# A side split's raw load moved to the end of the unit ahead, its store moved behind the unit's first half

## The chip, the cores and the metric

The kernel runs on one NeuronCore of one Trainium2 chip. The metric is the device time of a whole execution in microseconds, smaller being better. The kernel before took 1582.54 us (median of three runs, 1578.42 to 1582.68).

## What is computed

Windowed attention over 4 x 8 heads, 576 positions and head dimension 64 (window 64), whose output becomes a matrix x of 2304 rows by 512 columns. On it stands a mixture of eight experts, where every row goes through every expert and P holds the mixing weights, from an iterated row and column normalisation:

```python
def _moe_ref(x, w_gate, w1, w2):
    ...                                   # P: N x E, eight rounds of row and column scaling
    out = np.zeros((N, D), dtype=np.float32)
    for e in range(E):                    # E = 8
        h = np.maximum(x @ w1[e], 0.0)    # 512 -> 1024
        ye = h @ w2[e]                    # 1024 -> 512
        out += P[:, e:e + 1] * ye
    return out
```

Everything is float32. TensorE takes float32 operands as two rounded parts, a high one (the value cast to the type fp32r) and a low one (the value minus its high part); a product takes the three pairs high-high, high-low and low-high.

## The kernel before

The rows of x are worked in three passes of six tiles of 128 rows. Attention and pass 0 come first (up to about 650 us), then pass 1 and pass 2. The change is in pass 1 alone. A pass goes through 30 groups of 256 hidden columns; two groups make a unit `u` (15 units, 0 to 14).

Both matrix products of a unit are done by Strassen-like schemes of seven products on half blocks. `First` (class at L1031) is a group's product with w1, one block per group: seven steps numbered 1, 5, 6, 2, 7, 3, 4, each with six matmuls (L217). `Second` is the product with w2, two blocks per unit, `S[u][0]` and `S[u][1]`, with the same seven steps (L1160). The order of a pass is written out by hand in `flow`: F[2u+1], F[2u+2], S[u][0], S[u][1], then F[2u+3] and so on. Inside a block the steps go 6, 2, then step 1 of the next block, 7, 3, then step 5 of the next block, 4. So a unit is 28 products. Work on the other engines hangs on this order through `hook(block, step, f)`: `f` is issued right behind that step, and every engine (SP, which issues all DMAs, among them) works its own instructions strictly in the order of issue.

What hangs on it around the change:

- `load_w1` (L754), hooked on step 4 of every First block: five DMAs that refill the w1 buffer which that block has just finished with. SP waits there until TensorE is done with step 4.
- `next_pb` (L722), in every second unit: two DMAs of mixing weights, also on step 4 of a First block.
- Each unit needs seven parts of w2 (raw blocks, or sums of blocks kept in `w2d`). `load_w2` (L982) loads a part into one of four buffers `wr`; `split_w2` (L742, by `split_into`) makes the high part on ScalarE (L741) and the low part on GpSimd (L742). The load that reuses a buffer is issued just ahead of the next split, and SP waits in it for GpSimd's split of that buffer. The seven splits for the next unit, numbered 0 to 6 here, are issued at S[u][0] step 4, S[u][1] steps 6 and 2, F[2u+3] steps 1 and 5, S[u][1] step 4 and F[2u+3] step 6. The load issued with split n is the part for split n+3.
- `u2` (L1072): ScalarE's copy of bank b behind First step 6. Step 7 adds into bank b, so TensorE may not start it before that copy. It is issued behind split 5 on ScalarE.
- The side splits. In units 2 to 8 of pass 1 (`KEEP`), one part of unit 0 each is split ahead for pass 2: `load_kept` (L1002) loads the raw part into a buffer `ys`, `keep_split` (L1006 on ScalarE, L1007 on GpSimd) splits it into the second buffer `ys` and in place, `store_kept` (L1012) writes both halves to `w2keep` with two DMAs. There are two `ys` buffers, so the load of a unit reuses the buffer that the store of the unit before read. Pass 2 loads `w2keep` much later.

Of the kernel before, what the change touches and what calls it, by code (L numbers as in the profile page):

```python
# [21 lines left out]
def window_attention_sinkhorn_moe(ctx: ExitStack, tc: tile.TileContext, q, k, v, w_gate, w1, w2, out):  # L22
    nc = tc.nc
    B, H, S, D = q.shape
# [51 lines left out]
    def f32(ap):  # L76
        return ap.bitcast(F32)
# [3 lines left out]
    class Ring:  # L81
# [10 lines left out]
        def new(self):  # L92
            i = self.i % self.n
            self.i += 1
            pool = self.pool_a if i < self.na else self.pool_b
            return pool.tile(self.shape, self.dtype, tag=f"{self.name}_{i}", name=f"{self.name}_{i}")
# [226 lines left out]
    with tc.manual_schedule():  # L323
# [411 lines left out]
        def w2_block(u, part):  # L735
            e, c = groups[2 * u]
            src = w2[e, c * HD:(c + 2) * HD, :].rearrange("(g f p) (h d) -> p f g h d", g=2, f=2, h=2)
            return src[:, (1, 0, 0)[part], :, (0, 0, 1)[part], :]
# [202 lines left out]
        with ExitStack() as p3:  # L941
# [19 lines left out]
            KEEP = {u: k for u, k in zip(range(2, 9), ORDER)}  # L961
# [38 lines left out]
            def load_kept(part):  # L1000
                raw_k[part] = r = new("ys", [P, DM], F32R, 2)
                nc.sync.dma_start(out=f32(r), in_=w2_block(0, part) if part < 3 else w2d[0][:, part - 3])  # L1002

            def keep_split(part):
                r, h = raw_k.pop(part), new("ys", [P, DM], F32R, 2)
                nc.scalar.copy(out=h, in_=f32(r))  # L1006
                nc.gpsimd.tensor_tensor(out=r, in0=f32(r), in1=f32(h), op=ALU.subtract)  # L1007
                raw_k[part] = h, r

            def store_kept(part):  # L1010
                for x, t in enumerate(raw_k.pop(part)):
                    nc.sync.dma_start(out=w2keep[part][:, :, x, :], in_=f32(t))  # L1012
# [7 lines left out]
            def queue_w2(pu, ks):  # L1020
                if pu:
                    bulk.extend([lambda k=k: split_w2(*pu, ORDER[k]) for k in ks])
# [271 lines left out]
            for p, F, S, flow in plans:  # L1294
# [5 lines left out]
                def hook(blk, step, *fs):  # L1300
                    hooks.setdefault((blk, step), []).extend(fs)
# [20 lines left out]
                            hook(F[i + 3], 4, lambda p=p: next_pb(p + 1, 1))  # L1322
                for u in range(n_units - 1):
                    if p == 1 and u in KEEP:
                        hook(F[2 * u + 2], 4, lambda k=KEEP[u]: load_kept(k))
                        hook(S[u][0], 7, lambda k=KEEP[u]: keep_split(k))
                        hook(S[u][1], 2, lambda k=KEEP[u]: store_kept(k))
                    hook(S[u][0], 1, lambda s=S[u][0]: queue_w2(s.nxt, (0,)))
                    for st, k in ((1, 1), (5, 2), (6, 3), (2, 4), (7, 5), (3, 6)):
                        hook(S[u][1], st, lambda s=S[u][1], k=k: queue_w2(s.nxt, (k,)))  # L1330
# [113 lines left out]
```

## Time and profile before

| | us |
|---|---|
| median of three runs | 1582.54 (1578.42 to 1582.68) |
| the profiled execution | 1579.0 |
| its span, first to last instruction | 1577.3 |
| TensorE busy in the span | 1551.3 |
| ScalarE, VectorE, GpSimd busy | 760.6, 960.6, 991.8 |

The profile is of one execution. The time of that execution and its span differ by 1.7 us, which lies around the span. Matmuls overlap in the array, so a group's mean of one matmul (337 ns) isn't what one costs in a row: six of them, one product, take 1.04 us on the chain. A releaser named for an idle time is the event that came last by the profile.

### The profile page before, as it was taken

To read this page: it belongs to the slowest core of one execution; us is meant where nothing else is said; L and a number is where in the kernel's file an instruction comes from. 1 tells how busy PE (TensorE), PEld (TensorE's weight loads), DVE (VectorE), ACT (ScalarE), POOL (GpSimd) and SP (SyncE) were. 2 spreads that over 40 slices of the span, in tenths; PEclk is the share of its full clock that TensorE was granted. 3 is DMA by queue.
4 is the path that set the end of the run, shared out by engine and by line. 5 is a ranking of instruction groups with operands and counts; after the bars stand their busy time and mean duration, and the time that the engine had idled before them with its cause. 6 is when DMAs were issued, how large, how long until landed. Compare 5 with 4: busy or idle time off the path is not lost.

```text
span 1577.3 us, 26781 instructions
## 1 busy us (share of the span) xinstructions
PE 1551.3 (98%) x9665; PEld 1477.2 (94%) x9665; DVE 960.6 (61%) x1796; ACT 760.6 (48%) x1670; POOL 991.8 (63%) x925
## 2 busy tenths in 40 slices
PE   8999999999999999999999999999999999999998
PEld 6888889889988998999999999999999999999998
DVE  7666556665555455656655566576656576576566
ACT  6666535433443443365444444444464454444453
POOL 6244467676777677265566566657676657657665
PEclk9999999999999999999999999999999999999999
DMA  9876467567756756885665666556876556566552
GB/s 221 202 173 149 129 241 286 195 234 267 259 206 243 258 201 235 298 292 181 209 210 186 198 210 221 188 188 209 302 272 207 181 199 208 177 199 212 172 194 100
DMA packets 231233, 335.67 MB, mean 213 GB/s; under 512 B 70162, under 2 KB 153214, under 8 KB 227134
## 3 DMA queue, kind: packets, MB, share of 16 engines
q1 hardware_dynamic: 231102, 333.97, 65.4%
q8 instruction: 76, 1.25, 0.3%
q14 instruction: 55, 0.45, 0.1%
HBM read 236.34 MB, written 90.63 MB: 207 GB/s over the span
## 4 chain that ended last, share of the span: by engine, by line
PE 88%; DMA 5%; DVE 2%; issue 2%; POOL 1%; ACT 1%; SPq 1%; DVEq 0%; POOLq 0%; ACTq 0%
PE qb L217 17%; PE y L276 15%; PE qc L217 11%; PE qa L217 10%; PE qb L1160 10%; PE qa L1160 7%; PE qc L1160 7%; PE hp L562 3%; PE yp L576 3%; DMA wr<-in_moe_w_dram 2%; PE vp L479 1%; PE tp L390 1%; DMA wr<-w2d 1%; PE sp L410 1%; PE tp L464 1%
## 5 line engine op out<-in xcount | busy, mean ns | idle before, releaser
L217 PE MATMUL qb<-xc,w1c 128*128 128x384 f32 x1620 | 323.7, 337 | 12.7 <-ACT u L1072 12.1
L217 PEld LDWEIGHTS qb<-xc,w1c 128*128 128x128 f32 x1620 | 284.7, 188 | 17.3 <-ACT u L1072 15.3
L1046 POOL TENSOR_TENSOR G<-sm,G 128x384 fp32r<-128x384 f32 x176 | 179.0, 1017 | 183.0 <-ACT G L1042 180.8
L276 PE MATMUL y<-w2c,g 128*128 128x512 f32 x1080 | 251.0, 391 | 0.5 <-DVE acc L295 0.5
L276 PEld LDWEIGHTS y<-w2c,g 128*128 128x128 f32 x1080 | 201.9, 188 | 42.4 <-DVE acc L295 0.9
L217 PE MATMUL qc<-xc,w1c 128*128 128x384 f32 x1080 | 216.8, 340 | 0.0
L217 PE MATMUL qa<-xc,w1c 128*128 128x384 f32 x1080 | 213.6, 337 | 0.1
L217 PEld LDWEIGHTS qc<-xc,w1c 128*128 128x128 f32 x1080 | 194.0, 191 | 0.0
L217 PEld LDWEIGHTS qa<-xc,w1c 128*128 128x128 f32 x1080 | 190.3, 188 | 1.6 <-DMA w1c<-w1d 0.4
L1168 DVE TENSOR_TENSOR acc<-qb,acc 128x384 f32<-128x384 f32 x171 | 95.0, 556 | 123.2 <-PE qb L1160 110.7
L178 POOL TENSOR_TENSOR w2c<-stg,w2c 128x512 fp32r<-128x512 f32 x60 | 84.6, 1431 | 108.5 <-PE qb L217 95.9
L742 POOL TENSOR_TENSOR w2c<-wr,w2c 128x512 fp32r<-128x512 f32 x99 | 126.4, 1294 | 37.6 <-ACT w2c L741 32.9
L742 POOL TENSOR_TENSOR wp<-wr,wp 128x512 fp32r<-128x512 f32 x100 | 127.7, 1294 | 30.7 <-ACT wp L741 22.4
L1042 ACT CAST G<-sm 128x384 fp32r<-128x384 f32 x180 | 92.3, 514 | 65.5 <-DVE sm L1053 65.5
L1160 PE MATMUL qb<-G,w2c 128*128 128x384 f32 x552 | 111.2, 336 | 0.0
L1160 PE MATMUL qb<-G,wp 128*128 128x384 f32 x528 | 106.3, 336 | 0.0
L295 DVE SCALAR_TENSOR_TENSOR acc<-y,prob,acc 128x512 f32<-128x512 f32 x72 | 54.0, 749 | 73.6 <-PE y L276 73.0
L1160 PEld LDWEIGHTS qb<-G,w2c 128*128 128x128 f32 x552 | 97.7, 188 | 0.0
L1160 PEld LDWEIGHTS qb<-G,wp 128*128 128x128 f32 x528 | 93.4, 188 | 0.0
L1168 DVE TENSOR_TENSOR acc<-qc,acc 128x384 f32<-128x384 f32 x116 | 64.4, 555 | 41.3 <-PE qc L1160 40.6
L458 POOL TENSOR_TENSOR s<-s,rr 128x512 f32<-128x512 f32 x36 | 37.5, 1041 | 79.6 <-DVE rr L457 72.3
L1053 DVE TENSOR_TENSOR y<-qb,p 128x384 f32<-128x384 f32 x60 | 34.0, 566 | 78.4 <-PE qb L217 76.9
(213 smaller groups left out, 2937.9 us busy)
## 6 DMA issues: line engine op xcount, KB each, us to landing
w1c<-w1d SPq DMA_DIRECT2D x120, 512.0 KB, 6.4
w1d<-w1c SPq DMA_DIRECT2D x30, 1792.0 KB, 7.7
w1c<-w1d SPq DMA_DIRECT2D x180, 256.0 KB, 3.5
stg<-in_moe_w_dram SPq DMA_DIRECT2D x66, 512.0 KB, 4.1
wr<-w2d SPq DMA_DIRECT2D x114, 256.0 KB, 3.2
wr<-in_moe_w_dram SPq DMA_DIRECT2D x85, 256.0 KB, 3.7
w2d<-tf SPq DMA_DIRECT2D x30, 512.0 KB, 4.8
vs<-v SPq DMA_DIRECT2D x35, 128.0 KB, 4.1
```

Of the source, the lines that this page charges most:

```text
L178: nc.gpsimd.tensor_tensor(out=w[:, 1], in0=src[:, j], in1=f32(w[:, 0]), op=ALU.subtract)
L217: nc.tensor.matmul(bank, lhsT=w[:, ws, a, kk, :], rhs=xc[xs][:, b, kk, :], start=(first and j == 0), stop=(j == 5), skip_group_check=not f ...
L276: nc.tensor.matmul(yp, lhsT=g[:, a, o:o + P], rhs=w[:, x, :], start=(i == 0), stop=(i == 11))
L295: nc.vector.scalar_tensor_tensor(out=at, in0=yp, scalar=pr, in1=at, op0=ALU.mult, op1=ALU.add)
L458: nc.gpsimd.tensor_tensor(out=st, in0=st, in1=rr[:, :, None].to_broadcast([P, 4, P]), op=ALU.mult)
L562: nc.tensor.matmul(hp, lhsT=w1s[c][:, a, kk, :], rhs=xs[j][:, b, kk, :], start=(i == 0), stop=(i == 3 * KD - 1))
L576: nc.tensor.matmul(yp, lhsT=g[:, a, o * P:(o + 1) * P], rhs=w[:, x, :], start=(i == 0), stop=(i == 11))
L742: nc.gpsimd.tensor_tensor(out=t[:, :, 1, :], in0=r, in1=f32(t[:, :, 0, :]), op=ALU.subtract)
L1042: nc.scalar.copy(out=self.g[:, k, 0, :], in_=src)
L1046: eng.tensor_tensor(out=self.g[:, k, 1, :], in0=src, in1=f32(self.g[:, k, 0, :]), op=ALU.subtract)
L1160: nc.tensor.matmul(bank, lhsT=W[p, u, wp][:, g, y, cols], rhs=G7[p, 2 * u + g][:, gp, x, :], start=(start and j == 0), stop=(j == 5), skip ...
L1168: nc.vector.tensor_tensor(out=at, in0=src, in1=at, op=ALU.add)
```

## The change

Two hooks of the side splits move; their bodies are the same.

- The load of the raw part goes from F[2u+2] step 4 to S[u-1][1] step 4. It was issued behind that block's w1 load and mixing weights, one half unit ahead of its cast; it is now issued ahead of both w1 loads of the unit.
- The store goes from S[u][1] step 2 to S[u][0] step 4. The cast stays at S[u][0] step 7, so between cast and store there are now the products of S[u][0] step 3, S[u][1] step 5 and S[u][0] step 4; before there were two more, S[u][1] steps 6 and 2.

```diff
                 for u in range(n_units - 1):
                     if p == 1 and u in KEEP:
-                        hook(F[2 * u + 2], 4, lambda k=KEEP[u]: load_kept(k))
+                        hook(S[u - 1][1], 4, lambda k=KEEP[u]: load_kept(k))
                         hook(S[u][0], 7, lambda k=KEEP[u]: keep_split(k))
-                        hook(S[u][1], 2, lambda k=KEEP[u]: store_kept(k))
+                        hook(S[u][0], 4, lambda k=KEEP[u]: store_kept(k))
```

Nothing is added or removed: seven loads, seven casts, seven subtractions and fourteen stores stand on both sides.

## Rows read from the trace of the kernel before

**Rows 1.** The page: span, and TensorE's busy time.
```profile
span 1577.3 us, 26781 instructions
PE 1551.3 (98%) x9665; PEld 1477.2 (94%) x9665; DVE 960.6 (61%) x1796; ACT 760.6 (48%) x1670; POOL 991.8 (63%) x925
```

**Rows 2.** TensorE by unit: length, busy (instructions), granted clock, DMA share, GB/s.
```profile
731.15:760.41 29.26, 29.26 (x170) 1.00 0.62 199
760.41:794.14 33.73, 31.07 (x170) 0.95 0.63 198
794.14:824.92 30.78, 30.05 (x170) 1.00 0.64 204
985.79:1015.05 29.26, 29.26 (x170) 1.00 0.62 202
...
760.41:985.79 225.38, 212.68 (x1177) 208.81 (x1177) 131.70 (x252) 105.38 (x227) 142.10 (x128) 0.98 0.63 202
```

**Rows 3.** TensorE's waits, 745 to 971 us: total, times, longest.
```profile
PE qb L217 <- ACT u L1072: 12.1, 9, 2.8
PE qb L217 <- ACT qb L1060: 0.6, 2, 0.4
```

**Rows 4.** ScalarE's waits in the same stretch.
```profile
ACT ys L1006 <- DMA ys<-w2d: 19.5, 4, 5.7
...
ACT wp L741 <- DMA wr<-w2d: 17.2, 7, 3.2
ACT w2c L741 <- DMA wr<-w2d: 16.8, 7, 3.0
ACT ys L1006 <- DMA ys<-in_moe_w_dram: 12.7, 3, 5.1
```

**Rows 5.** Timeline of unit 2, all engines: start, length, idle before and releaser.
```profile
754.56 1.78 SPq L1002 DMA_DIRECT2D ys<-in_moe_w_dram  x1
766.60 0.37 SPq L982 DMA_DIRECT2D wr<-in_moe_w_dram  x1
767.02 1.18 SPq L1012 DMA_DIRECT2D w2keep<-ys  x2
...
762.06 0.62 ACT L1006 CAST ys<-ys 128x512 fp32r<-128x512 f32 x1 [5.13 <-DMA ys<-in_moe_w_dram]
770.58 0.62 ACT L741 CAST w2c<-wr 128x512 fp32r<-128x512 f32 x1 [1.51 <-DMA wr<-in_moe_w_dram]
771.11 0.47 ACT L1072 COPY u<-qb 128x384 f32<-128x384 f32 x1
...
762.76 1.30 POOL L1007 TENSOR_TENSOR ys<-ys,ys 128x512 fp32r<-128x512 f32 x1 [4.27 <-DMA wr<-in_moe_w_dram]
...
771.63 1.81 PE L217 MATMUL qb<-xc,w1c 128*128 128x384 f32 x6 [2.66 <-ACT u L1072]
```

**Rows 6.** Timeline of unit 1, which has no side split, all engines.
```profile
730.50 0.32 SPq L982 DMA_DIRECT2D wr<-w2d  x1
731.75 0.38 SPq L982 DMA_DIRECT2D wr<-in_moe_w_dram  x1
738.00 1.58 SPq L982 DMA_DIRECT2D wr<-w2d  x2
743.94 8.10 SPq L754 DMA_DIRECT2D w1c<-w1d  x7
...
735.97 1.14 ACT L741 CAST w2c<-wr 128x512 fp32r<-128x512 f32 x2
737.70 0.48 ACT L1072 COPY u<-qb 128x384 f32<-128x384 f32 x1 [0.58 <-PE qb L217]
...
729.19 2.54 POOL L742 TENSOR_TENSOR wp<-wr,wp 128x512 fp32r<-128x512 f32 x2
...
739.55 1.20 PE L217 MATMUL qb<-xc,w1c 128*128 128x384 f32 x6
```

**Rows 7.** Landings: line 982 in unit 1; raw loads (1002); stores (1012).
```profile
DMA to landing us min/median/max: 2.6/3.1/5.7
...
DMA to landing us min/median/max: 6.2/7.2/7.5
...
DMA to landing us min/median/max: 3.1/3.8/4.3
```

**Rows 8.** The chain of waits: part loads behind a store (first) and behind w1.
```profile
865.42 5.19 DMA wr<-w2d
756.44 6.29 DMA wr<-in_moe_w_dram
```

## The prediction

> **What bounds the kernel now.** I read the page first. TensorE is busy for 1551.3 of 1577.3 us [rows 1], so all that can be won is TensorE's idle time and stretches in which its clock is low. Then I laid windows over pass 1, each from the first product of F[2u+3] in one unit to the same product of the next. A unit without a side split takes 29.26 us, all of it busy, both ahead of the seven side splits and behind them; with one it takes 33.73 us in unit 2 and 30.78 in unit 3 [rows 2]. Over the seven units together it is 225.38 us against 7 x 29.26 = 204.82: **20.56 us are lost there**. TensorE is busy for 212.68 of them [rows 2], so 12.70 us are idle and 7.86 us are the same number of products done more slowly. The windows say why: the mean granted clock is 0.95 in unit 2 and 1.00 in the units without a side split [rows 2], that is, for part of the unit TensorE stood at 1.2 instead of 2.4 GHz, behind the stall. Lost busy time per idle time is 7.86 / 12.70 = 0.62.
>
> The waits name the releaser. Of the 12.70 us idle, 12.1 end at ScalarE's copy `u` (L1072) and 0.6 at its copy of bank b [rows 3]. ScalarE in turn waits 19.5 + 12.7 = 32.2 us, seven times, for the raw part of the side split, and, after that, about as long for the parts of w2 [rows 4]. Unit 2 shows how one leads to the other [rows 5]. SP issues the raw load at 754.56, behind both w1 loads; ScalarE sits for 5.13 us until it has landed and casts at 762.06; GpSimd subtracts at 762.76, and only behind that come its splits of parts 0, 1 and 2. Each of these frees a `wr` buffer, so the load for split 5 goes out at 766.60; the cast of split 5 waits for it until 770.58; the copy `u` stands behind it at 771.11, and TensorE's step 7 starts at 771.63 after 2.66 us idle. In unit 1, which has no side split, the splits on GpSimd start at 729.19, the loads for splits 4 and 5 go out at 730.50 and 731.75, their casts run at 735.97 without a wait, and `u` at 737.70 waits for TensorE, not the other way [rows 6].
>
> **The early load: takes 20.56 us away.** In the phase of unit 1 the raw load is now reached between the two part loads that begin at 738.00, and SP is then free until the w1 load at 743.94 [rows 6]. The two part loads end at 739.58, so there are 4.36 us of SP's time for an issue that takes at most 1.78 us [rows 5, 6]: what it is moved past (ten w1 pieces, the mixing weights, one part load) isn't held. Its longest landing was 7.5 us [rows 7], behind the w1 pieces; even with that it is there at about 746 in the phase of unit 1, while the cast is due 29.26 us after 727.6 (5.13 before 762.06 less the same 29.26), at 756.9. So it has 11 us to spare, and all 32.2 us of waiting for raw parts go. If that cover were gone, the wait would come back at the old price. The new wait is for the `ys` buffer: SP waits in the load until the store ahead has landed, and behind it stand a part load and both w1 loads. The store goes out by 731.7 (next part) and lands in at most 4.3 us [rows 7], at 736.0, 2.4 us before SP gets there. Price: nothing.
>
> **The cast and the subtraction stay**, 0.62 us on ScalarE and 1.30 on GpSimd [rows 5]. In unit 1 ScalarE has free time before its copies. GpSimd hasn't: the subtraction goes in at 729.19 and pushes the three splits behind it, so the load for split 4 goes out at about 731.8 instead of 730.50, and the one for split 5 at 733.05 instead of 731.75.
>
> **The store, two products earlier.** It now stands on SP ahead of the load for split 4, before it stood behind the load for split 5. It waits for GpSimd's subtraction, at 730.5; what is queued behind it is the load for split 4, which waits for split 0, the next instruction on GpSimd, until 731.7. The two issues take 1.18 us [rows 5] and fit between. SP loses nothing. What it does cost is the data in front of the two loads: 2 x 256 KB. No row shows these two loads behind a store; the bounds are 3.1 us, the median landing of part loads in unit 1 [rows 7], and 5.19 us, a part load right behind a store [rows 8]. I take the upper end, since it is the same kind of load at the same place. Then part 4 lands at 737.0 and part 5 at 733.05 + 5.19 = 738.24; the cast of split 5 takes 0.57 (half of 1.14) and `u` 0.48 [rows 6], so `u` ends at 739.29. TensorE's step 7 starts at 739.55 in unit 1 [rows 6]: it fits with 0.26 us to spare, and with the lower end `u` isn't later than TensorE lets it be, at 738.18. Price: nothing at either end, but near the edge at one.
>
> Here a rule speaks against the change. A load right behind a store took 5.19 us, against 3.1 for loads with nothing ahead [rows 7, 8]. The Trainium skill, "DMA: Bandwidth & Descriptors", section "Queues, rings and completion order", says that each DMA engine takes its descriptors in the order of the ring, so a store put in front is in front for good; by its fabric ceiling of 435 GB/s, 512 KB are an estimated 1.2 us, less than the 2.1 that these rows show. By the page the load for split 4 would land at 736.1, by the rows at 737.0; the sum is the same with both.
>
> **The sum.** The profiled execution took 1579.0 us: 1579.0 - 20.56 = 1558.4. The median of the runs shown lies 3.5 us above that execution, and the fastest run 0.6 below; the runs fall to both ends of that spread, so I put the new time midway, 1.6 us up: **1560.0 us**.
>
> **Rivals.** *Part of the stall stays.* If the load for split 5 lands as late as one behind the w1 pieces did, 6.29 us [rows 8], it lands at 739.34, `u` ends at 740.39, and TensorE starts step 7 at 740.43, 0.88 us late. Over seven units that is 6.2 us idle, and with 0.62 for the clock 10.0 us: 1568.4, or 1570.0 on the scale of my number. For it: the margin of 0.26 us is thin and the store's bytes do lie in front. Against: the w1 pieces that made 6.29 are over by then, as the landings of 3.1 us in unit 1 show.
>
> *The change does nothing*: if the raw load were still held on SP, by a part load that waits for GpSimd, until the w1 loads' time, the casts would wait as before: 1579 to 1583. Against it: SP stands idle for over 4 us at that place [rows 6].
>
> *Slower: the store in front costs more than the raw load did.* The place is the same, split 5's cast ahead of `u`. To lose the 20.56 us again and 4.7 more takes 25.3 / 7 / 1.62 = 2.23 us idle in each unit, which the load for split 5 reaches when it lands 7.64 us after its issue, and from there the kernel is slower; at 8.0 us it would be 1588.0 by the profiled time, 1590 on my scale. The longest part load that I found took 6.29 us [rows 8] and the raw loads behind ten w1 pieces 7.5 [rows 7], so it needs more than any row shows.
>
> **How the numbers follow.** The whole loss comes back: 0.79. Part of it: 0.13. Nothing: 0.04. Slower: 0.04. A measurement of this kernel can tell about 0.3% from no change, 4.7 us. The first two are both faster by more than that, 0.91 with a little taken off for a stall that stays nearly whole; within it 0.05; slower 0.04. The range begins at 1556.5, the fastest run less the loss (1557.8) with 1.3 for windows read to about 0.2 us in each unit, and reaches to 1571, the end of the partial case.
>
> **What would show it.** Right: units 2 to 8 at 29.3 us each, the granted clock 1.00 in each, no wait of ScalarE for `ys`, no wait of TensorE for `u`. The store: part loads behind it land in 3.1 to 5.2 us, and ScalarE waits for parts 4 and 5 but not beyond TensorE's slack. Wrong: TensorE still idle before step 7 with `u` behind a cast that waits for a part, or SP waiting in line 1002 for a store to land while w1 loads stand behind it.

## The result, and the profile after

The changed kernel took **1558.43 us** (median of five runs, 1558.13 to 1559.22) against 1582.54 us (1578.42 to 1585.00). The ratio is 0.9855, 95% interval 0.9837 to 0.9874. The forecast was 1560.0 us, with a range of 1556.5 to 1571.0. The profiled execution took 1558.66 us, its span is 1556.7 us against 1577.3 [rows 1]: 20.6 us shorter, where the loss read from the windows was 20.56 us.

The page of the kernel after, first the span, then busy time (share) and instructions by engine:

```profile
span 1556.7 us, 26797 instructions
PE 1544.7 (99%) x9665; PEld 1474.3 (95%) x9665; DVE 966.4 (62%) x1796; ACT 760.9 (49%) x1670; POOL 990.8 (64%) x925
```

TensorE's windows over units 2 and 8, and over all seven (length, busy time and instructions; granted clock, DMA share and GB/s at the end; the last line has all engines):

```profile
760.48:789.73 29.25, 29.25 (x169) 1.00 0.68 223
...
936.01:965.27 29.26, 29.26 (x170) 1.00 0.63 207
...
760.48:965.27 204.79, 204.79 (x1178) 204.79 (x1178) 130.96 (x252) 104.13 (x223) 139.91 (x127) 1.00 0.69 221
```

These answer rows 2. A unit with a side split now takes what a unit without one takes, TensorE is busy for all of it, and the clock is 1.00 throughout. ScalarE and GpSimd work about as long as before (104.13 and 139.91 us, against 105.38 and 142.10 [rows 2]); only the waiting has gone. TensorE has no wait at all in this stretch, where it had those of rows 3. ScalarE's waits there (total, times, longest):

```profile
ACT qb L1060 <- PE qa L217: 18.5, 7, 2.6
...
ACT u L1072 <- PE qb L217: 3.9, 7, 0.9
ACT wp L741 <- DMA wr<-in_moe_w_dram: 0.7, 1, 0.7
ACT w2c L741 <- DMA wr<-in_moe_w_dram: 0.4, 1, 0.4
```

The waits for `ys` of rows 4 are gone, and those for parts of w2 are 1.1 us in all. ScalarE now waits for TensorE, seven times for the product that `u` copies. The direction has turned round.

Unit 2 in the timeline of the kernel after, for rows 5 (SP, ScalarE, GpSimd, TensorE; start, length, idle before and its releaser):

```profile
754.70 1.13 SPq L982 DMA_DIRECT2D wr<-in_moe_w_dram  x1
757.55 2.81 SPq L1012 DMA_DIRECT2D w2keep<-ys  x2
761.11 0.34 SPq L982 DMA_DIRECT2D wr<-w2d  x1
762.35 0.38 SPq L982 DMA_DIRECT2D wr<-in_moe_w_dram  x1
...
767.71 1.09 SPq L1002 DMA_DIRECT2D ys<-w2d  x1
...
756.91 0.62 ACT L1006 CAST ys<-ys 128x512 fp32r<-128x512 f32 x1
765.30 1.14 ACT L741 CAST w2c<-wr 128x512 fp32r<-128x512 f32 x2
767.03 0.48 ACT L1072 COPY u<-qb 128x384 f32<-128x384 f32 x1 [0.59 <-PE qb L217]
...
758.51 1.31 POOL L1007 TENSOR_TENSOR ys<-ys,ys 128x512 fp32r<-128x512 f32 x1
...
768.88 1.20 PE L217 MATMUL qb<-xc,w1c 128*128 128x384 f32 x6
```

The cast runs at 756.91 without a wait, 5.15 us earlier than in rows 5; the loads for splits 4 and 5 leave SP at 761.11 and 762.35, their casts run at 765.30 without a wait, and TensorE's step 7 starts on time at 768.88. The raw part for the next unit leaves SP at 767.71.

### The profile page after: what moved, and what is told of

Read it like the earlier page. It is cut to its first block, busy times and chain, and to the rows that moved or that the text cites. A ratio compares the mean times of both kernels' runs of the same rounds, so it can differ in the third digit from the quotient of the medians.

```text
span 1556.7 us, 26797 instructions
## 1 busy us (share of the span) xinstructions
PE 1544.7 (99%) x9665; PEld 1474.3 (95%) x9665; DVE 966.4 (62%) x1796; ACT 760.9 (49%) x1670; POOL 990.8 (64%) x925
## 4 chain that ended last, share of the span: by engine, by line
PE 97%; DVE 1%; ACT 1%; DMA 0%; issue 0%; SPq 0%; DVEq 0%
PE qb L217 18%; PE y L276 15%; PE qa L217 12%; PE qb L1160 12%; PE qc L217 12%; PE qa L1160 8%; PE qc L1160 8%; PE hp L562 3%; PE yp L576 3%; PE vp L479 1%; PE tp L390 1%; PE sp L410 1%; PE tp L464 1%; DMA q<-in_q_dram 0%; PE hp L519 0%; PE idle L614 0%
## 5 line engine op out<-in xcount | busy, mean ns | idle before, releaser
L217 PE MATMUL qc<-xc,w1c 128*128 128x384 f32 x1080 | 213.0, 336 | 0.0
L217 PEld LDWEIGHTS qc<-xc,w1c 128*128 128x128 f32 x1080 | 190.2, 188 | 0.0
L1053 POOL TENSOR_TENSOR r<-sm,r 128x384 f32<-128x384 f32 x60 | 61.0, 1017 | 28.8 <-ACT u L1072 13.9
```

Source lines behind the costliest of these rows:

```text
L217: nc.tensor.matmul(bank, lhsT=w[:, ws, a, kk, :], rhs=xc[xs][:, b, kk, :], start=(first and j == 0), stop=(j == 5), skip_group_check=not f ...
L1053: eng.tensor_tensor(out=dst, in0=x, in1=y, op=op)
```

## The experiments

Theory: the loss was ScalarE sitting in front of a raw part that had not landed, with everything behind that cast late; it is won back as soon as the part lands ahead of its cast, however that comes about, and the store's place doesn't matter then. The main rivals: the store had to move as well; the load has to be ahead of both w1 loads; the side splits still cost something; or the stores stand at the edge in front of the part loads, as my sum had it. The diffs of `e1`, `e4`, `e5` and `e8` are against the kernel after, the others against the kernel before; all intervals are of the ratio to the kernel before.

### The load alone

```diff
-                        hook(S[u][0], 4, lambda k=KEEP[u]: store_kept(k))
+                        hook(S[u][1], 2, lambda k=KEEP[u]: store_kept(k))
```

> The load of the raw part at the end of the unit ahead, the store left at S[u][1] step 2. Theory (the whole gain is ScalarE's wait for the raw part, 32.2 us before): 1558 to 1560 us, units 2 to 8 at 29.3 us each, no wait for ys. Rival (the store has to move too, since the next load reuses the buffer that the store reads, and SP holds a part load and both w1 loads behind that wait): the store is issued at about 735.5 in the phase of unit 1 and lands 3.8 to 4.3 us later, the load is reached at 738.4, so SP is held for 1 to 2 us in each unit; if that reaches TensorE, 3 to 20 us are lost, 1561 to 1579 us.

Measured: 1558.59 us (1558.50 to 1558.81), ratio 0.9859 (0.9844 to 0.9873). The load alone is the whole gain. ScalarE's only waits for DMA in the stretch:

```profile
ACT w2c L741 <- DMA wr<-w2d: 5.0, 4, 1.4
ACT wp L741 <- DMA wr<-w2d: 3.8, 3, 1.4
```

Seven waits, one in each unit, for the part that split 6 takes, whose load stands right behind the store there. They don't reach TensorE. SP wasn't held by the `ys` buffer either: the load went out at 767.83 in this kernel too, 0.12 us later than in the kernel after.

### The store alone

```diff
-                        hook(S[u][1], 2, lambda k=KEEP[u]: store_kept(k))
+                        hook(S[u][0], 4, lambda k=KEEP[u]: store_kept(k))
```

> The store at S[u][0] step 4, the load left where it was, behind the w1 load of F[2u+2] step 4. Theory (the store's place gives nothing): not faster than before, 1579 us; and since the store now stands ahead of the part loads for splits 4 and 5, which TensorE is already late for, up to 1.2 us later in each unit, with 0.62 for the clock up to 14 us more, so 1579 to 1593 us. Rival (part of the gain comes from the store): below 1574 us.

Measured: 1575.13 us (1570.94 to 1578.62), ratio 0.9966 (0.9953 to 0.9980). **A miss for the theory**: 5.5 us faster than the 1580.68 us of the kernel before beside it, neither the same nor slower; nor is it below 1574 us, where the rival had it. The waits for the raw part are as long as before, and TensorE still waits for `u`:

```profile
ACT ys L1006 <- DMA ys<-w2d: 20.1, 4, 5.8
ACT ys L1006 <- DMA ys<-in_moe_w_dram: 12.7, 3, 5.0
ACT wp L741 <- DMA wr<-w2d: 12.0, 7, 3.3
ACT w2c L741 <- DMA wr<-w2d: 11.7, 6, 3.7
ACT wp L741 <- DMA wr<-in_moe_w_dram: 1.2, 3, 0.5
ACT w2c L741 <- DMA wr<-in_moe_w_dram: 1.0, 2, 0.7
...
PE qb L217 <- ACT u L1072: 10.1, 7, 2.6
```

But TensorE waits seven times, not eleven [rows 3]. The seven are one in each unit, at step 7. The eleven were six of that kind and five that came later in a unit, 1.58 us together, and these five are gone. The experiment "The store behind all part loads" asks where they came from.

### The load ahead of one w1 load

The load stays on the same hook, in front of `load_w1` instead of behind it.

```diff
-                        hook(F[2 * u + 2], 4, lambda k=KEEP[u]: load_kept(k))
+                        hooks[F[2 * u + 2], 4].insert(0, lambda k=KEEP[u]: load_kept(k))
```

> The load stays on F[2u+2] step 4 but is issued ahead of that block's w1 load instead of behind it; the store is left at S[u][1] step 2. SP then reaches it before it waits for TensorE's step 4: about 746.2 in unit 2, 8 us earlier than before, and the cast is due at 756.9. Theory (what counts is that the raw part lands ahead of its cast; the wait on TensorE and five w1 pieces in front of it were what made it late): 1558 to 1561 us, no wait for ys. Rival (it has to go in front of both w1 loads, because the first w1 load's data are in front of it as well): waits for ys of 1 us or more stay, 1563 to 1575 us.

Measured: 1558.60 us (1558.32 to 1558.91), ratio 0.9859 (0.9844 to 0.9873). The raw load of unit 2 on SP, and the cast on ScalarE:

```profile
746.05 0.43 SPq L1002 DMA_DIRECT2D ys<-in_moe_w_dram  x1
751.08 2.22 SPq L754 DMA_DIRECT2D w1c<-w1d  x5
...
756.68 0.62 ACT L1006 CAST ys<-ys 128x512 fp32r<-128x512 f32 x1
...
DMA to landing us min/median/max: 7.1/7.3/7.3
```

The landing takes 7.1 to 7.3 us here, as long as before [rows 7], with the five pieces of the first w1 load right ahead of it; in the kernel after, where both w1 loads come behind it, it takes 3.5 to 4.0. It doesn't matter: SP reaches the load 5 us before the w1 load for which it waits on TensorE, and that is enough. The end of the unit ahead isn't needed.

### The old load, a later cast

```diff
-                        hook(S[u][0], 7, lambda k=KEEP[u]: keep_split(k))
-                        hook(S[u][1], 2, lambda k=KEEP[u]: store_kept(k))
+                        hook(S[u][1], 7, lambda k=KEEP[u]: keep_split(k))
+                        hook(F[2 * u + 3], 7, lambda k=KEEP[u]: store_kept(k))
```

> The load stays where it was before, behind the w1 load of F[2u+2] step 4; the cast and the subtraction go from S[u][0] step 7 to S[u][1] step 7, six products later, and the store to F[2u+3] step 7. Theory (only the time between the load's landing and its cast counts, not the load's place in SP's order): the raw part lands at about 762 in unit 2, and the cast is due at about 762.5 there, so ScalarE waits for ys 0 to 1 us in each unit and TensorE doesn't: 1558 to 1562 us. Rival (the raw load's 256 KB and its issue, behind the w1 loads and ahead of the part loads, are themselves what delays the unit): 1566 to 1580 us.

Measured: 1558.72 us (1558.16 to 1560.98), ratio 0.9869 (0.9852 to 0.9886). The load is where it was before and lands as slowly (median 7.1 us); no cast of a raw part waits for it. So neither the load's place on SP nor its bytes in front of the part loads were what cost time. It was the distance from landing to cast. (The store had to move behind the later cast; that move alone gives 5.3 us of the 21.8, as the next experiment shows.)

### The store behind all part loads

```diff
-                        hook(S[u][1], 2, lambda k=KEEP[u]: store_kept(k))
+                        hook(F[2 * u + 3], 7, lambda k=KEEP[u]: store_kept(k))
```

> Load and cast where they were before; the store goes later, to F[2u+3] step 7, behind all part loads of the unit. It asks why moving the store ahead, alone, took 5.5 us off the kernel before. Theory (before, the store stood in front of the load for split 6, and ScalarE waited for that part behind u, which kept TensorE slow or idle a second time): a store behind all part loads takes the same wait away, 1573 to 1577 us, and ScalarE's waits for parts fall from 40 us to under 30. Rival (the gain came from the part loads 4 and 5, or from chance in the clock after a stall): 1579 to 1584 us.

Measured: 1575.23 us (1571.45 to 1576.22), ratio 0.9963 (0.9951 to 0.9974). Moving the store later gives the same as moving it ahead. What the two have in common is that it no longer stands in front of the load for split 6, where the kernel before has it. ScalarE's waits for parts fall from 17.2 + 16.8 us, and 3.5 + 3.2 for the other source, to 25.6 us here and 25.9 us with the store ahead:

```profile
ACT wp L741 <- DMA wr<-w2d: 10.7, 6, 2.8
ACT w2c L741 <- DMA wr<-w2d: 9.8, 5, 3.9
ACT wp L741 <- DMA wr<-in_moe_w_dram: 2.9, 3, 2.1
ACT w2c L741 <- DMA wr<-in_moe_w_dram: 2.2, 3, 1.2
...
PE qb L217 <- ACT u L1072: 10.9, 5, 2.6
```

Unit 3 shows it: the cast of split 6 and TensorE's second stall in the kernel before, then the same cast with the store ahead.

```profile
805.68 0.62 ACT L741 CAST w2c<-wr 128x512 fp32r<-128x512 f32 x1 [2.87 <-DMA wr<-w2d]
807.49 1.31 PE L217 MATMUL qb<-xc,w1c 128*128 128x384 f32 x6 [0.17 <-ACT qb L1060]
...
802.55 0.62 ACT L741 CAST w2c<-wr 128x512 fp32r<-128x512 f32 x1 [0.50 <-DMA wr<-w2d]
```

So in the kernel before the store did cost something: behind a late `u`, split 6 waited again for a part that stood behind the store (5.19 us to land, [rows 8]), and the copies behind it were late a second time. In a unit that is on time the same wait is hidden, as in the first experiment. How the 5.3 to 5.5 us divide stays open: TensorE's idle time falls by 1.8 to 2.6 us, and the rest is busy time, of which the last section shows two parts: fewer restarts, and the clock, which differs from run to run.

### Fewer side splits

```diff
-            KEEP = {u: k for u, k in zip(range(2, 9), ORDER)}
+            KEEP = {2: 0}
...
-                nc.sync.dma_start(out=f32(t), in_=w2keep[part])
+                nc.sync.dma_start(out=f32(t), in_=w2keep[0])
```

> The changed kernel with the side split of unit 2 alone; those of units 3 to 8, with their loads, casts, subtractions and stores, are left out, and pass 2 loads the one part seven times. Theory (with the load early the side splits cost TensorE nothing): 1557.5 to 1559.5 us, within 1 us of the changed kernel. Rival (they still cost ScalarE, GpSimd or DMA time that reaches TensorE): 1550 to 1556 us.

This kernel leaves out six of the seven parts that pass 2 needs, so only its time is of use. Measured: 1558.23 us (1557.85 to 1558.60), ratio 0.9856 (0.9841 to 0.9871). Six side splits fewer, with some 8 us of GpSimd's time, are worth 0.2 us, less than the runs differ. Nothing more is to be had from the side splits.

### Two and four stores

```diff
                     nc.sync.dma_start(out=w2keep[part][:, :, x, :], in_=f32(t))
+                    for m in range(3):
+                        nc.sync.dma_start(out=w2more[part][:, m, :, x, :], in_=f32(t))
```

(with one extra copy instead of three in the first of the two)

> The changed kernel with every store of a side split issued twice, the second copy to another place in memory: 1 MB instead of 512 KB in front of the part loads for splits 4 and 5. Theory (the part loads have the slack of TensorE's step 7 behind the copy u, about 1.3 us, and the store in the changed kernel uses little of it): the issues put the load for split 4 back by about 1.1 us and the data by up to 1.5 us, so u is up to 1.3 us late and TensorE hardly waits: 1558 to 1562 us. Rival (the store already stands at the edge, as the prediction's upper end had it with 0.26 us to spare): TensorE idle about 1 us in each of seven units, 1566 us or more.

> The changed kernel with every store issued four times, 2 MB in front of the part loads for splits 4 and 5. Theory (the prediction's slower rival has the right mechanism and only its size was far from real): the load for split 4 goes out 3 us later and its data lie behind 2 MB, some 5 us at the 350 GB/s of busy stretches, so part 5 lands 2 to 4 us too late and TensorE waits 0.7 to 3 us in each unit: 1566 to 1592 us, with TensorE's waits at step 7 for u. Rival (stores in front don't delay loads, since what they write and what loads read go side by side): under 1562 us.

Measured: 1558.79 us (1558.08 to 1559.50), ratio 0.9866 (0.9851 to 0.9882), with 1 MB, and 1572.32 us (1570.51 to 1575.97), ratio 0.9949 (0.9931 to 0.9967), with 2 MB. Twice the store is still hidden; four times isn't. With 2 MB, SP's stores and the loads for splits 4 and 5 in unit 2, the casts of these splits, and TensorE's waits in the stretch (the lines of this kernel are a few higher: 742 is the cast, 1075 the copy `u`, 218 the First product):

```profile
757.24 0.52 SPq L1013 DMA_DIRECT2D w2keep<-ys  x1
757.81 1.94 SPq L1015 DMA_DIRECT2D w2more<-ys  x3
760.23 0.55 SPq L1013 DMA_DIRECT2D w2keep<-ys  x1
760.82 2.25 SPq L1015 DMA_DIRECT2D w2more<-ys  x3
763.17 0.66 SPq L983 DMA_DIRECT2D wr<-w2d  x1
763.93 0.64 SPq L983 DMA_DIRECT2D wr<-in_moe_w_dram  x1
...
768.41 1.34 ACT L742 CAST w2c<-wr 128x512 fp32r<-128x512 f32 x2 [3.31 <-DMA wr<-w2d]
...
PE qb L218 <- ACT u L1075: 11.5, 7, 2.8
```

The slower rival's mechanism is real, but its place is one cast ahead of the one I named: ScalarE waits for the part of split 4, once in each unit, and split 5 follows without a wait. The cast is 3.11 us later than in the kernel after (768.41 against 765.30), and 2.06 us of that is SP, which is still issuing stores when it would issue the load (763.17 against 761.11). But 2 MB in front cost 13.9 us over the kernel after; the 512 KB that the change puts there cost nothing that can be measured.

## Why the prediction was right

**The stall and its price.** Right in sum: the windows gave 20.56 us, and the profiled spans differ by 20.6. That the loss comes back whole, the clock's part with it, follows from the windows after. The reading of the 7.86 us as the clock's alone was wrong: 2.4 of them arose in units whose granted clock was 1.00, as rows 2 show for unit 3 already, 0.79 us busier at 1.00 (last section). The sum isn't touched by that, but the rivals were priced with the 0.62 that came of it, that is 1.62 us lost for 1 us idle, and no such factor held: the profiled spans with 10.1, 10.9 and 11.5 us idle (store alone, store late, four stores) are 12.5, 17.1 and 16.1 us longer than that of the kernel after, which is 1.24, 1.57 and 1.40. (And the slower rival's sum at 8.0 us gives 1587.8, not 1588.0.)

**The early load.** Right in its price. SP reaches it between the last two part loads (767.71, which is 738.4 in the phase of unit 1, as worked out), and it holds up no w1 load. Its landing, instead of 6.2 to 7.5 us [rows 7]:

```profile
DMA to landing us min/median/max: 3.5/4.0/4.0
```

The cover for the `ys` buffer was thinner than I had it. The stores land 2.8 to 6.6 us after their issue, median 4.5, where I took 4.3 at most; in unit 2 even 6.6 us behind the second store's issue at 759.9 still leave 1.2 us until SP reaches the next raw load at 767.71, where I had 2.4. SP doesn't wait for a store in line 1002 in this stretch. The experiments say more than the prediction did: this place has more room than is needed, since a load that leaves five of the ten w1 pieces in front, or a later cast, gives the same time.

**The store: the price was right, a term was not.** I took 5.19 us as the landing of a part load behind the store, and had 0.26 us to spare. The part loads of unit 2 that begin from 760 to 766 us, the store's data in front, landed in (minimum, median, maximum):

```profile
DMA to landing us min/median/max: 3.1/3.4/3.8
```

Those for splits 4 to 6 in the other units took 3.0 to 4.2 us. The nearer end was the lower one, 3.1 [rows 7]. The two ends of the sum gave the same time, so the number didn't suffer, but "near the edge" was wrong: doubling the store still cost nothing. A detail explains part of it. I had both stores wait for GpSimd's subtraction. The first writes the high half and needs only ScalarE's cast, and it begins at 757.55, ahead of the subtraction; so half of the 512 KB is on its way 3.6 us before the load for split 4. The load that took 5.19 us [rows 8] had both halves issued right in front of it. The rule of the Trainium skill ("DMA: Bandwidth & Descriptors", section "Queues, rings and completion order") that each DMA engine takes its descriptors in the order of the ring agrees with these rows: with 2 MB issued right in front, the loads for splits 4 and 5 of unit 2 landed in 5.1 to 5.2 us.

**"Price: nothing" for the store's place** was right beside an early load and wrong by itself: with the old load, taking the store from in front of split 6's part is worth 5.5 us. Of the 24 us it isn't an addition, because the load's move hides that wait too.

**The median.** This step failed, by 1.6 us. I put the new time midway in the spread of the runs before, as if the spread would stay. The spread was part of the loss. The kernel before ran 14 times beside the experiments with the late cast, the late store and the two and four stores. Four of these runs, the fastest and the slowest among them, with the mean granted clock of each execution:

| kernel before, us | granted clock |
|---|---|
| 1577.31 | 0.995 |
| 1580.84 | 0.995 |
| 1583.27 | 0.993 |
| 1585.14 | 0.994 |

The six of the 14 that are above 1581 us show 0.993 or 0.994, the eight below it 0.995 to 0.997. With the stalls gone the five runs lie within 1.1 us, at 0.997 to 0.999. So the medians moved by 24.1 us where the profile showed 20.6: the profiled execution was one of the luckier ones of the kernel before, and the right step was to give the new kernel the time of the profile, 1558.4, with no share of the spread.

## What to carry to other kernels

Where an engine works its instructions in order, a cast that waits for a load is paid by everything behind it, and the engine that is late at the end of that chain can be one that never touches the data: follow the wait back to its first late transfer. What counts is that the transfer lands ahead of its reader; an issue in front of the one instruction for which the issuing queue waits, or a reader a few products later, does as well as an issue far ahead. And a spread between runs can itself be a symptom of stalls, so a change that removes them takes the spread away with them.

## What the runs showed of the hardware

TensorE's stalls cost busy time beside the idle time, in two ways, and only one of them is the clock. Three stalls and the windows of their units: unit 6 and unit 8 of the kernel before, with 2.01 and 2.36 us idle, and unit 2 of the kernel with the store alone moved, with 2.55 us idle (the matmul lines show the product behind the stall):

```profile
900.45 1.32 PE L217 MATMUL qb<-xc,w1c 128*128 128x384 f32 x6 [2.01 <-ACT u L1072]
889.88:922.97 33.09, 31.08 (x170) 0.95 0.62 201
```

```profile
964.83 1.31 PE L217 MATMUL qb<-xc,w1c 128*128 128x384 f32 x6 [2.36 <-ACT u L1072]
953.90:985.79 31.89, 29.53 (x169) 1.00 0.62 200
```

```profile
771.95 1.32 PE L217 MATMUL qb<-xc,w1c 128*128 128x384 f32 x6 [2.55 <-ACT u L1072]
760.83:792.92 32.09, 29.54 (x169) 1.00 0.65 209
```

The first way is the restart. At a granted clock of 1.00 the product behind a stall takes 1.31 or 1.32 us; in a row, where products overlap, one takes 1.04. That is the 0.27 us or so by which the busy time of these units is up (29.53 and 29.54 against 29.26). The second is the clock. The shortest of the three stalls was followed by a granted clock of 0.95 over the unit and cost 1.82 us of busy time, the two longer ones only the restart. The length of a stall alone didn't settle its price.

So the 7.86 us that the kernel before was busier over its seven units, beside 12.70 us idle, are of two kinds. Units 3, 5, 7 and 8 stand at 1.00 and are 2.40 us busier than four units without a stall, with nine restarts; units 2, 4 and 6 stand at 0.95 and are 5.46 us busier. With 0.27 us off for a restart in each of these three, an estimate of 4.7 us is left for the clock. In the profiled run with the store alone the clock was 1.00 in all seven units, and the 1.9 us more busy time beside 10.1 us idle are seven restarts.
